# Another route to the low weights, and the rounded FFN activations on ScalarE outside the main heads

## The chip, the cores and the metric

One core of one Trainium2 chip. The metric is device microseconds of one execution, the median of three runs. The engines are TensorE (PE in the profile, its weight loads PEld), VectorE (DVE), ScalarE (ACT), GpSimd (POOL) and SyncE, whose queue (SPq) issues nearly all transfers. Each engine takes its instructions in the order in which they were laid down when the kernel was built.

## The reference

Forgetting attention, then a feed-forward net (FFN) over all tokens:

```python
scores = scale * np.matmul(q, k.transpose(0, 1, 3, 2))      # 8 batches x 8 heads, S=576, D=64
cum = np.cumsum(np.log(np.clip(f, 0.0001, 1.0)), axis=-1)
scores = scores + cum[:, :, :, None] - cum[:, :, None, :]    # causal
attn = softmax(scores);  x = attn @ v                        # tokens 4608 x 512
h = x @ w_in;  g = np.maximum(0.01 * h, h)                   # w_in 512 x 2048
out = g @ w_out                                              # w_out 2048 x 512
```

w_in and w_out are float64.

## The kernel before

The large products run as fp32r matmuls on pairs of a rounded high part and a low part: h is the sum of xh·win_h, xh·win_l and xl·win_h; o, the output, that of gh·wout_h, gh·wout_l and gl·wout_h, where gh is g rounded to fp32r and gl = g − gh.

**The weights** come in 16 pieces of 128 x 1024 (even numbers w_in, odd ones w_out), each as pairs of int32 words of the float64: `hi` (sign, exponent, 20 mantissa bits) and `lo` (32 more). `fetch_weight` issues the two transfers of a piece (L163) into one of two `wraw` buffers; `load_weight` makes the high weights (win_h, wout_h) and the low ones (win_l, wout_l) with two ScalarE and five VectorE instructions (L177 to L191). A `wraw` buffer is free for piece n+2 when the last of them has run; `wt`, a single buffer, is free for piece n+1 when its last reader has.

**The first 145 us** (the loop over `steps`) run an early attention over the first 256 tokens of three batches: in each of 12 steps two heads' scores (`sce`, whose max and exponentials `ze` go over DVE L301 and ACT L305), the division by their sums (L313), transposes (`tre`, copied out by ACT L325 as `pte`), attention times values (`ave`), and its split into `xh` (ACT L338) and `xl` (DVE L339). One weight piece is converted in each of the first eight steps, two in each of the last four. After each step `fill` puts in FFN work from the generator `ffn` (`FQ` sets how much: none in the first four steps); `warm` matmuls on zeros stand in the first six steps.

**From about 145 to 1095 us** the main heads run (`heads[0]` is True), with FFN work between them; there gl is made by GpSimd. **After 1095 us** only FFN is left. `ffn` makes, for each of 18 groups of 256 tokens and 8 pieces of w_in: `h` (24 matmuls), `g` by ScalarE (L629), `gh` by VectorE (L632), `gl` (L634: by VectorE where heads[0] is False), and then the 12 `o` matmuls of the piece before it (`second`).

A scheduler in the framework lays down the order on each engine when the kernel is built, from dependencies and its own estimate of durations; so a change of one instruction's engine or length can move others.

Of the kernel before, what the change touches and what calls it, by code (L numbers as in the profile page):

```python
# [8 lines left out]
F32 = mybir.dt.float32  # L9
F32R = mybir.dt.float32r  # L10
I32 = mybir.dt.int32
U32 = mybir.dt.uint32
AF = mybir.ActivationFunctionType
ALU = mybir.AluOpType
# [24 lines left out]
def forgetting_attention_ffn(ctx, tc, qT, kT, v4, vr, f, w_in, w_out, out):  # L39
# [6 lines left out]
    nc = tc.nc  # L46
# [60 lines left out]
    def matmul(*args, **kw):  # L107
        work[0] += 1
        nc.tensor.matmul(*args, **kw)  # L109
# [50 lines left out]
    def fetch_weight(n):  # L160
        raw = raws[n] = one.tile([P, 2, 4 * P, 2], I32, tag=RAWS[n % 2], name=f"wraw_{n}")
        for k, src in enumerate(wpieces[n][0]):
            nc.sync.dma_start(raw[:, k].rearrange("p w two -> p (w two)"), src)  # L163

    def load_weight(n):


        loaded.append(n)
        _, wh, wl = wpieces[n]
        wh, wl = (w.rearrange("p c f -> p (c f)") for w in (wh, wl))  # L170
        if n not in raws:
            fetch_weight(n)
        raw = raws[n].rearrange("p m w two -> p (m w) two")
        lo, hi = raw[:, :, 0], raw[:, :, 1]
        t = one.tile([P, 8 * P], I32, tag="vs", name=f"wt_{n}")
        tf = t.bitcast(F32)
        first = nc.scalar.activation(tf, hi.bitcast(F32), AF.Prelu, scale=REBIAS, alpha=SIGN)  # L177
        if n == 0:
            tc.keep_in_program_order(first)
        first = nc.vector.tensor_scalar(t, t, 3, None, op0=ALU.logical_shift_left)  # L180
        if n == 0:
            tc.keep_in_program_order(first)
        nc.scalar.copy(wh, tf)
        nc.vector.tensor_scalar(hi, t, -0x800000, None, op0=ALU.bitwise_and)
        rest = lo.bitcast(F32)
        nc.vector.scalar_tensor_tensor(
            rest, lo.bitcast(U32), 2.0**-52, hi.bitcast(F32), op0=ALU.mult, op1=ALU.mult
        )
        hi = hi.bitcast(F32)
        nc.vector.tensor_tensor(hi, tf, wh.bitcast(F32), op=ALU.subtract)  # L190
        nc.vector.tensor_tensor(wl, hi, rest, op=ALU.add)  # L191

    def weights(n):
        while len(loaded) < min(n, len(wpieces)):
            load_weight(len(loaded))
# [383 lines left out]
    def fetch_group(n):  # L579
        if n not in groups and n not in staged and (n + 1) * T <= ready[0]:  # L580
            xs = staged[n] = one.tile([P, NCC, T], F32R, tag="b4", name=f"xs_{n}", bufs=B4)
            since[n] = work[0]
            nc.sync.dma_start(xs.bitcast(F32), xd[:, n * T:(n + 1) * T].rearrange("(c p) t -> p c t", p=P))
# [8 lines left out]
    def ffn():  # L592
        pending = None
        half = NFC // 2
        order = [(0, 0, HP), (1, 0, HP), (0, HP, half), (1, HP, half)]
        order += [(n, 0, half) for n in range(2, NG)]
        for at, (n, p0, p1) in enumerate(order):
            while (n + 1) * T > ready[0]:
                yield False
            if n not in groups:  # L600
                if n not in staged:
                    fetch_group(n)
                near[0] = True
                while n not in groups:
                    yield False
            acc = [None, None]
            for p in range(p0, p1):
                while len(loaded) < 2 * (p + 1):
                    yield False
                near[0] = p == p1 - 1  # L610
                xh, xl = groups[n]
                terms = [
                    (x, c, w, xx) for c in range(NCC)
                    for x, (w, xx) in enumerate(((win_h[p], xh), (win_l[p], xh), (win_h[p], xl)))
                ]
                if n >= 2:
                    terms.sort(key=lambda y: y[0])
                ph = psum.tile([P, 2, T], F32, tag="h", name=f"h_{n}_{p}")
                for e in range(2):
                    fs = slice(e * P, (e + 1) * P)  # L620
                    for y, (x, c, w, xx) in enumerate(terms):
                        matmul(
                            ph[:, e, :], w[:, c, fs], xx[:, c, :],
                            start=y == 0, stop=y == len(terms) - 1,
                        )
                    if e == 0:
                        yield True
                g = one.tile([P, 2, T], F32, tag="b2", name=f"g_{n}_{p}", bufs=B2)
                nc.scalar.activation(g, ph, AF.Prelu, alpha=0.01)  # L629
                gh = one.tile([P, 2, T], F32R, tag="b2", name=f"gh_{n}_{p}", bufs=B2)  # L630
                gl = one.tile([P, 2, T], F32R, tag="b2", name=f"gl_{n}_{p}", bufs=B2)
                nc.vector.tensor_copy(gh, g)  # L632
                eng = nc.gpsimd if heads[0] else nc.vector
                eng.tensor_tensor(gl, g, gh.bitcast(F32), op=ALU.subtract)  # L634
                yield True
                if pending is not None:
                    yield from second(*pending)
                if p0 < p and at + 1 < len(order):
                    fetch_group(order[at + 1][0])
                pending = (n, p, p0, p1, gh, gl, acc)  # L640
        yield from second(*pending)

    def second(n, p, p0, p1, gh, gl, acc):
        for k in range(T // P):
            if p == p0:
                acc[k] = psum.tile([P, DM], F32, tag=f"o{k}", name=f"o_{n}_{k}_{p}", bufs=1)
            ts = slice(k * P, (k + 1) * P)
            for e in range(2):
                fc_ = 2 * p + e
                for x, (gg, w) in enumerate(((gh, wout_h[p]), (gh, wout_l[p]), (gl, wout_h[p]))):  # L650
                    matmul(
                        acc[k], gg[:, e, ts], w[:, e, :],
                        start=(fc_ == 2 * p0 and x == 0), stop=(fc_ == 2 * p1 - 1 and x == 2),
                    )
            if p == p1 - 1 < NFC // 2 - 1:
                tag, m = PARTS[2 * n + k]
                o = parts[n, k] = one.tile([P, DM], F32, tag=tag, name=f"part_{n}_{k}", bufs=m)
                nc.scalar.copy(o, acc[k])
            elif p == p1 - 1:
                if (n, k) in parts:  # L660
                    o = parts[n, k]
                    nc.vector.tensor_tensor(o, acc[k], o, op=ALU.add)
                else:
                    o = one.tile([P, DM], F32, tag="ost", name=f"ost_{n}_{k}", bufs=2)
                    nc.scalar.copy(o, acc[k])
                for x, row, m in segments(n * T // P + k):
                    nc.sync.dma_start(out[row:row + m, :], o[x:x + m])
            yield True

    parts = {}  # L670
    quanta = ffn()
    heads = [False]
    ready, used, credit = [0], [0], [0.0]
# [127 lines left out]
```

## Time and profile before

| | us |
|---|---|
| median of 3 runs (lowest, highest) | 1209.06 (1208.9, 1209.14) |
| the profiled execution: time, span in the profile | 1208.6, 1206.8 |
| busy in the span: PE, DVE, ACT, POOL | 1192.4, 625.9, 636.0, 461.0 |
| busy from 0 to 165 us: PE, DVE, ACT | 159.2, 126.8, 114.1 |

The profiled execution has 1.8 us outside the span, and the median of the runs is 0.46 us above it. Matmuls are pipelined and their ends are modelled, so a PE that is "busy" may still be held back. A group's idle time is the engine's idle time just before it.

### The profile page before, as it was taken

To read this page: it belongs to the slowest core of one execution; us is meant where nothing else is said; L and a number is where in the kernel's file an instruction comes from. 1 tells how busy PE (TensorE), PEld (TensorE's weight loads), DVE (VectorE), ACT (ScalarE), POOL (GpSimd) and SP (SyncE) were. 2 spreads that over 40 slices of the span, in tenths; PEclk is the share of its full clock that TensorE was granted. 3 is DMA by queue.
4 is the path that set the end of the run, shared out by engine and by line. 5 is a ranking of instruction groups with operands and counts; after the bars stand their busy time and mean duration, and the time that the engine had idled before them with its cause. 6 is when DMAs were issued, how large, how long until landed. Compare 5 with 4: busy or idle time off the path is not lost.

```text
span 1206.8 us, 22499 instructions
## 1 busy us (share of the span) xinstructions
PE 1192.4 (99%) x7812; PEld 1068.2 (89%) x7812; DVE 625.9 (52%) x1685; ACT 636.0 (53%) x1633; POOL 461.0 (38%) x473
## 2 busy tenths in 40 slices
PE   9999999999999999999999999999999999999998
PEld 6677888888899999999999999999999999998997
DVE  6988665565656555454445444444443434553221
ACT  5876665666755565555554545455444445552011
POOL 2000255555455445354435344444354543531000
PEclk9999999999999999999999999999999999999999
DMA  5555433334342333323332323232223222211000
GB/s 169 184 173 176 133 100 100 102 108 122 103 137 81 82 99 101 96 71 97 89 94 75 88 63 101 65 100 60 68 85 93 58 72 80 80 58 52 12 18 18
DMA packets 82129, 110.55 MB, mean 92 GB/s; under 512 B 20640, under 2 KB 51728, under 8 KB 82016
## 3 DMA queue, kind: packets, MB, share of 16 engines
q1 hardware_dynamic: 82016, 109.12, 31.0%
q8 instruction: 62, 1.02, 0.3%
q14 instruction: 51, 0.42, 0.1%
HBM read 65.32 MB, written 18.58 MB: 70 GB/s over the span
## 4 chain that ended last, share of the span: by engine, by line
PE 92%; DVE 2%; DMA 2%; ACT 2%; issue 1%; SPq 0%; POOL 0%; ACTq 0%; DVEq 0%; POOLq 0%
PE h L109 33%; PE o L109 32%; PE tr L113 8%; PE av L109 8%; PE sc L109 7%; PE sce L109 2%; DMA wraw<-in_w_in 2%; PE warm L109 2%; PE ave L109 1%; DVE fixed_z L412 0%; ACT wt L177 0%; PE tre L113 0%; ACT g L629 0%; DVE gh L632 0%; DVE pl L464 0%
## 5 line engine op out<-in xcount | busy, mean ns | idle before, releaser
L634 POOL TENSOR_TENSOR gl<-g,gh 128x512 fp32r<-128x512 f32 x113 | 148.7, 1316 | 275.6 <-DVE gh L632 270.7
L109 PE MATMUL o<-wout_h,gh 128*128 128x512 f32 x576 | 231.3, 402 | 0.0
L109 PE MATMUL o<-wout_h,gl 128*128 128x512 f32 x576 | 227.0, 395 | 0.6 <-DVE gl L634 0.6
L109 PE MATMUL o<-wout_l,gh 128*128 128x512 f32 x576 | 227.1, 394 | 0.0
L418 ACT ACTIVATE fixed_z<-fixed_z,max 128x192 f32<-128x192 f32 (+3 forms) x272 | 161.0, 592 | 100.3 <-DVE max L412 98.1
L109 PE MATMUL h<-xh,win_h 128*128 128x256 f32 x1152 | 206.5, 286 | 0.5 <-ACT xh L338 0.4
L462 ACT CAST ph<-tr 128x192 fp32r<-128x192 f32 (+3 forms) x360 | 126.9, 373 | 151.5 <-PE tr L113 99.5
L109 PE MATMUL h<-xh,win_l 128*128 128x256 f32 x1152 | 200.7, 283 | 0.0
L412 DVE CUSTOM_DVE_ANT_0 fixed_z<-sc,tri 128x192 f32<-128x192 f32 (+3 forms) x272 | 122.5, 452 | 150.6 <-PE sc L109 147.7
L629 ACT ACTIVATE g<-h 128x512 f32<-128x512 f32 x144 | 85.8, 596 | 214.6 <-PE h L109 202.9
L632 DVE CAST gh<-g 128x512 fp32r<-128x512 f32 x144 | 74.4, 517 | 209.8 <-ACT g L629 208.4
L464 DVE TENSOR_TENSOR pl<-tr,ph 128x384 fp32r<-128x384 f32 (+3 forms) x296 | 137.6, 467 | 82.2 <-ACT ph L462 81.1
L109 PEld LDWEIGHTS h<-xh,win_h 128*128 128x128 f32 x1152 | 170.9, 190 | 7.1 <-ACT xh L338 1.2
L109 PEld LDWEIGHTS h<-xh,win_l 128*128 128x128 f32 x1152 | 165.1, 191 | 0.8 <-DVE win_l L191 0.3
L109 PE MATMUL h<-xs,win_h 128*128 128x256 f32 x1024 | 164.4, 283 | 0.0
L113 PE MATMUL tr<-ident_r,fixed_z 128*128 128x128 f32 x888 | 145.2, 273 | 3.2 <-DVE ph L469 1.7
L109 PEld LDWEIGHTS h<-xs,win_h 128*128 128x128 f32 x1024 | 140.9, 191 | 0.0
L109 PEld LDWEIGHTS o<-wout_h,gl 128*128 128x128 f32 x576 | 108.2, 188 | 25.1 <-DVE gl L634 0.8
L113 PEld LDWEIGHTS tr<-ident_r,fixed_z 128*128 128x128 f32 x888 | 107.8, 140 | 24.6 <-ACT rb L541 5.2
L109 PEld LDWEIGHTS o<-wout_l,gh 128*128 128x128 f32 x576 | 108.7, 189 | 15.6 <-issue 0.2
L109 PEld LDWEIGHTS o<-wout_h,gh 128*128 128x128 f32 x576 | 108.9, 189 | 14.8
L109 PE MATMUL sc<-m,s 128*128 128x288 f32 (+1 forms) x336 | 120.6, 364 | 0.2
(111 smaller groups left out, 1684.4 us busy)
## 6 DMA issues: line engine op xcount, KB each, us to landing
raw<-in_kT SPq DMA_DIRECT2D x64, 144.0 KB
m<-m SPq DMA_DIRECT2D x64, 144.0 KB
wraw<-in_w_in SPq DMA_DIRECT2D x16, 512.0 KB
wraw<-in_w_out SPq DMA_DIRECT2D x16, 512.0 KB
fixed_vm<-in_v SPq DMA_DIRECT2D x64, 128.0 KB
xs<-xd SPq DMA_DIRECT2D x16, 512.0 KB
out<-ost SPq DMA_DIRECT2D x28, 256.0 KB
raw<-in_qT SPq DMA_DIRECT2D x40, 144.0 KB
```

Of the source, the lines that this page charges most:

```text
L109: nc.tensor.matmul(*args, **kw)
L113: nc.tensor.transpose(*args)
L412: nc.vector.tensor_tensor_reduce(out=z[:, a:b], in0=ps[:m, :b - a], in1=tri[:m, at:at + b - a], scale=-SCALE, scalar=3.0e38 if x == 0 else ...
L418: nc.scalar.activation(z, z, AF.Exp, bias=h["max"][:m, last:last + 1], scale=-1.0, accum_out=fixed["sum" + "ab"[s // 2 % 2]][:m, i, s % 2: ...
L462: nc.scalar.copy(strided(ph, run), source(ps, run))
L464: nc.vector.tensor_tensor(strided(pl, run), source(ps, run), strided(ph, run).bitcast(F32), op=ALU.subtract)
L629: nc.scalar.activation(g, ph, AF.Prelu, alpha=0.01)
L632: nc.vector.tensor_copy(gh, g)
L634: eng.tensor_tensor(gl, g, gh.bitcast(F32), op=ALU.subtract)
```

## The change

`load_weight` makes the low weights in another way. Before, the rest of rounding (tf − wh) and the scaled low word were computed apart and added. Now bit 2 is set in `t` (it stands for half of what `t` cuts off), the 9 lowest bits of `hi` and the 23 highest of `lo` are joined to one signed 32-bit integer, and this is multiplied by 2^-43 and the power of two of the weight. There are again five VectorE instructions, but of other kinds: before two of one input and three of two; now three of one input and two of two. The low weights no longer read the high ones.

`ffn` makes `gh` with ScalarE's copy where `heads[0]` is False (31 of 144 pieces: 12 ahead of the main heads, 19 behind them) and by VectorE otherwise.

```diff
-        first = nc.vector.tensor_scalar(t, t, 3, None, op0=ALU.logical_shift_left)
+        first = nc.vector.tensor_scalar(
+            t, t, 3, 4, op0=ALU.logical_shift_left, op1=ALU.bitwise_or
+        )
...
         nc.scalar.copy(wh, tf)
+        nc.vector.tensor_scalar(hi, hi, 23, None, op0=ALU.logical_shift_left)
+        nc.vector.scalar_tensor_tensor(
+            lo, lo, 9, hi, op0=ALU.logical_shift_right, op1=ALU.bitwise_or
+        )
         nc.vector.tensor_scalar(hi, t, -0x800000, None, op0=ALU.bitwise_and)
-        rest = lo.bitcast(F32)
         nc.vector.scalar_tensor_tensor(
-            rest, lo.bitcast(U32), 2.0**-52, hi.bitcast(F32), op0=ALU.mult, op1=ALU.mult
-        )
-        hi = hi.bitcast(F32)
-        nc.vector.tensor_tensor(hi, tf, wh.bitcast(F32), op=ALU.subtract)
-        nc.vector.tensor_tensor(wl, hi, rest, op=ALU.add)
+            wl, lo, 2.0**-43, hi.bitcast(F32), op0=ALU.mult, op1=ALU.mult
+        )
...
-                nc.vector.tensor_copy(gh, g)
+                (nc.vector.tensor_copy if heads[0] else nc.scalar.copy)(gh, g)
```

Lines behind L184 stand two further down in the new kernel (L185 is ScalarE's copy to the high weights; L186, L187, L190 and L191 are VectorE's new steps; L301 becomes L303, L629 L631, L634 L636, and the new L634 is gh). The order of the instructions moves on all engines up to the end of the early steps; from the first main head on it is the same on PE, DVE, ACT, POOL and SP, but for gh in the tail. Three places:

VectorE in the fourth early step (batch 0, head pair 3), before. Piece 2 is win_1; `xl_0_154<-ave_0_1` is the second quarter of xl of the first token group. Rows carry tile numbers.

```order
L186 SCALAR_TENSOR_TENSOR wraw_2_367<-wraw_2_367 128x1024
L301 ISA ze_1_0_0_504,maxe_1_0_496<-sce_1_0_0_498,tri_157 128x128
L301 ISA maxe_1_0_496 128x1
L190 TENSOR_TENSOR wraw_2_367<-wt_2_370,win_h_1_99 128x1024
L339 TENSOR_TENSOR xl_0_154<-ave_0_1_407,xh_0_153 128x256
L191 TENSOR_TENSOR win_l_1_107<-wraw_2_367 128x1024
L224 TENSOR_SCALAR fc_143<-fc_143 128x576
```

The same place now:

```order
L180 TENSOR_SCALAR wt_2_370<-wt_2_370 128x1024
L186 TENSOR_SCALAR wraw_2_367<-wraw_2_367 128x1024
L187 SCALAR_TENSOR_TENSOR wraw_2_367<-wraw_2_367 128x1024
L190 TENSOR_SCALAR wraw_2_367<-wt_2_370 128x1024
L191 SCALAR_TENSOR_TENSOR win_l_1_107<-wraw_2_367 128x1024
L226 TENSOR_SCALAR fc_143<-fc_143 128x576
L341 TENSOR_TENSOR xl_0_154<-ave_0_1_407,xh_0_153 128x256
```

All five steps of piece 2 now stand in a row, and xl is behind them, no longer between them.

ScalarE where the first FFN pieces come in (batch 1, head pairs 0 and 1), before:

```order
L629 ACTIVATE g_0_0_593<-h_0_0_568 128x512
L305 ACTIVATE ze_1_1_0_643,sume_1_1_636<-ze_1_1_0_643,maxe_1_1_635 128x128
L305 ACTIVATE ze_1_1_2_646,sume_1_1_636<-ze_1_1_2_646,maxe_1_1_635 128x128
L177 ACTIVATE wt_5_680<-wraw_5_677 128x1024
L183 CAST wout_h_2_116<-wt_5_680 128x1024
L629 ACTIVATE g_0_1_624<-h_0_1_599 128x512
L305 ACTIVATE ze_1_1_1_660,sume_1_1_636<-ze_1_1_1_660,maxe_1_1_635 128x256
L305 ACTIVATE ze_1_1_3_663,sume_1_1_636<-ze_1_1_3_663,maxe_1_1_635 128x256
L325 COPY pte_1_0_0_692<-tre_1_0_0_688 128x384
L325 COPY pte_1_0_1_698<-tre_1_0_1_694 128x384
```

The same place now:

```order
L631 ACTIVATE g_0_0_593<-h_0_0_568 128x512
L307 ACTIVATE ze_1_1_0_643,sume_1_1_636<-ze_1_1_0_643,maxe_1_1_635 128x128
L634 CAST gh_0_0_595<-g_0_0_593 128x512
L307 ACTIVATE ze_1_1_2_646,sume_1_1_636<-ze_1_1_2_646,maxe_1_1_635 128x128
L177 ACTIVATE wt_5_680<-wraw_5_677 128x1024
L327 COPY pte_1_0_0_692<-tre_1_0_0_688 128x384
L631 ACTIVATE g_0_1_624<-h_0_1_599 128x512
L307 ACTIVATE ze_1_1_1_660,sume_1_1_636<-ze_1_1_1_660,maxe_1_1_635 128x256
L307 ACTIVATE ze_1_1_3_663,sume_1_1_636<-ze_1_1_3_663,maxe_1_1_635 128x256
L185 CAST wout_h_2_116<-wt_5_680 128x1024
L327 COPY pte_1_0_1_698<-tre_1_0_1_694 128x384
L634 CAST gh_0_1_626<-g_0_1_624 128x512
```

gh is a new row, the first pte moves ahead of g, and the high weights' copy moves behind it, ahead of the second pte.

VectorE where pieces come two to a step (piece 10 is win_5; batch 2, head pair 1), before:

```order
L301 ISA ze_2_1_0_1129,maxe_2_1_1121<-sce_2_1_0_1123,tri_157 128x128
L301 ISA maxe_2_1_1121 128x1
L301 ISA ze_2_1_2_1132,maxe_2_1_1121<-sce_2_1_2_1124,tri_157 128x128
L301 ISA maxe_2_1_1121 128x1
L180 TENSOR_SCALAR wt_10_1156<-wt_10_1156 128x1024
L184 TENSOR_SCALAR wraw_10_1153<-wt_10_1156 128x1024
L634 TENSOR_TENSOR gl_1_0_1052<-g_1_0_1049,gh_1_0_1051 128x512
```

The same place now:

```order
L180 TENSOR_SCALAR wt_10_1156<-wt_10_1156 128x1024
L186 TENSOR_SCALAR wraw_10_1153<-wraw_10_1153 128x1024
L187 SCALAR_TENSOR_TENSOR wraw_10_1153<-wraw_10_1153 128x1024
L190 TENSOR_SCALAR wraw_10_1153<-wt_10_1156 128x1024
L303 ISA ze_2_1_0_1129,maxe_2_1_1121<-sce_2_1_0_1123,tri_157 128x128
L303 ISA maxe_2_1_1121 128x1
L303 ISA ze_2_1_2_1132,maxe_2_1_1121<-sce_2_1_2_1124,tri_157 128x128
L303 ISA maxe_2_1_1121 128x1
L191 SCALAR_TENSOR_TENSOR win_l_5_111<-wraw_10_1153 128x1024
L636 TENSOR_TENSOR gl_1_0_1052<-g_1_0_1049,gh_1_0_1051 128x512
```

Four of the five steps of piece 10 have moved ahead of the maxima of the step's scores; in SP's queue the transfers of piece 10 have moved from behind the loads of the first main head to right behind those of piece 9.

## The prediction, made before the changed kernel ran

> **What bounds the kernel now.** I read the page first, then busy times by stage, then PE's waits, and then the chain and the queues of the stages where PE waits. The page:
>
> ```profile
> span 1206.8 us, 22499 instructions
> ...
> PE 1192.4 (99%) x7812; PEld 1068.2 (89%) x7812; DVE 625.9 (52%) x1685; ACT 636.0 (53%) x1633; POOL 461.0 (38%) x473
> ```
>
> PE is busy in 99% of the span; 14.4 us are left in which it stands. The stages (start:end, length, then busy time and instructions of PE, PEld, DVE, ACT, POOL, then PE's granted clock, DMA share, GB/s):
>
> ```profile
> 0.00:165.00 165.00, 159.15 (x919) 124.21 (x920) 126.79 (x280) 114.06 (x272) 23.00 (x42) 0.99 0.50 163
> 165.00:1095.00 930.00, 925.09 (x6218) 846.54 (x6217) 473.52 (x1362) 507.09 (x1337) 433.24 (x430) 1.00 0.31 87
> 1095.00:1207.00 112.00, 108.20 (x681) 97.48 (x679) 25.59 (x43) 14.88 (x25) 4.80 (x2) 0.99 0.08 26
> 35.00:50.00 15.00, 13.38 (x65) 8.86 (x65) 13.42 (x32) 12.75 (x33) 0.00 (x0) 0.89 0.57 173
> 93.00:100.00 7.00, 6.35 (x36) 4.52 (x35) 4.32 (x12) 5.15 (x13) 0.00 (x0) 1.00 0.50 179
> 109.00:114.00 5.00, 4.25 (x27) 2.89 (x26) 3.36 (x8) 3.70 (x8) 0.00 (x0) 1.00 0.61 213
> 127.00:130.00 3.00, 2.31 (x15) 1.51 (x14) 2.93 (x8) 2.46 (x6) 0.88 (x4) 1.00 0.82 278
> ```
>
> Up to 165 us PE stands for 165 − 159.15 = 5.85 us; VectorE is busy 126.8 and ScalarE 114.1, so neither fills the stage, and what the change can move there is PE's waits. From 35 to 50 us PE stands for 15 − 13.38 = 1.62 us and has 0.89 of its clock, another 0.11 x 15 = 1.65. In the last three rows, 0.65, 0.75 and 0.69 are lost. In the other stages 4.9 and 3.8 us are lost; the order of no engine changes in the main heads, so I leave them as they are. PE's own waits (us in total, times, longest) name those who end them:
>
> ```profile
> PE ave L109 <- ACT pte L325: 0.9, 2, 0.6
> ...
> PE sce L109 <- DVE maxe L301: 0.8, 1, 0.8
> PE tre L113 <- DVE xl L339: 0.7, 2, 0.4
> PE o L109 <- DVE gl L634: 0.6, 1, 0.6
> ```
>
> All four are small steps of the early stage that stand in a queue behind conversions of weights.
>
> **The change, part by part.** First the sizes, from the groups of 0 to 165 us (count, then busy us and mean ns, then idle before) and two from all of ScalarE:
>
> ```profile
> L186 DVE SCALAR_TENSOR_TENSOR wraw<-wraw 128x1024 f32<-128x1024 uint32 x16 | 19.6, 1222 | 0.3
> ...
> L184 DVE TENSOR_SCALAR wraw<-wt 128x1024 int32<-128x1024 int32 x16 | 11.0, 688 | 0.3
> L180 DVE TENSOR_SCALAR wt<-wt 128x1024 int32<-128x1024 int32 x16 | 11.0, 688 | 3.3 <-ACT wt L177 3.3
> ...
> L190 DVE TENSOR_TENSOR wraw<-wt,wout_h 128x1024 f32<-128x1024 f32 x8 | 10.1, 1266 | 1.6 <-ACT wout_h L183 1.2
> ...
> L190 DVE TENSOR_TENSOR wraw<-wt,win_h 128x1024 f32<-128x1024 f32 x8 | 9.8, 1223 | 0.1
> ...
> L191 DVE TENSOR_TENSOR win_l<-wraw 128x1024 fp32r<-128x1024 f32 x8 | 9.7, 1216 | 0.0
> ...
> L183 ACT CAST win_h<-wt 128x1024 fp32r<-128x1024 f32 x8 | 8.4, 1047 | 1.9 <-DVE wt L180 1.8
> ...
> L632 DVE CAST gh<-g 128x512 fp32r<-128x512 f32 x14 | 6.8, 489 | 9.2 <-ACT g L629 8.8 <-ACT pte L325 0.2
> ```
>
> ```profile
> L374 ACT CAST m<-raw 64x576 fp32r<-64x576 f32 x64 | 43.0, 671 | 1.8 <-DMA raw<-in_kT 0.2
> ...
> L462 ACT CAST ph<-tr 128x512 fp32r<-128x512 f32 x64 | 37.4, 584 | 12.0 <-PE tr L113 11.0
> ```
>
> *VectorE, per piece.* Out go 688 + 688 + 1222 + 1245 (mean of 1266 and 1223) + 1216 = 5059 ns. In come L180 with a second operation in it, and the mask, both as before at 688; two of two inputs at 1222 (L187, L191); and the shift of `hi`, which reads every other word. No row reads one input with such a stride; the bounds are 688 (L184, which writes with that stride) and 1222. I take 688, since L184 is the nearer row: 4508 ns, 0.55 us less per piece, 8.8 us in 16. At 1222 the saving is 0.02 us per piece. [...]
>
> *gh.* 12 casts leave VectorE ahead of the heads, 12 x 0.49 = 5.9 us. On ScalarE one costs between 584 ns (512 columns out of PSUM, L462) and 671 (576 columns, L374); from 1047 at 1024 columns and 671 at 576, 0.84 ns a column gives 617 at 512, which I take: 12 x 0.62 = 7.4 us. So by 165 us VectorE goes from 126.8 to 112, ScalarE from 114 to 121.5. gl no longer waits across engines for VectorE's own cast but for ScalarE's; in the early stage its `o` stands a whole FFN piece behind `h`, and that piece's matmuls hide the 0.13 us.
>
> *The start, 33 to 48 us.* The chain of waits there, in order of time (start, us, what), then VectorE's queue and one row of PE (the `ave` of the fourth head pair; start, us, engine, line):
>
> ```profile
> 38.75 0.38 DVE fc L224
> ...
> 40.40 5.87 DMA wraw<-in_w_in
> ...
> 46.38 1.17 ACT wt L177
> ...
> 47.93 0.27 ACT xh L338
> ...
> 48.24 0.74 PE h L109 x4
> ```
>
> ```profile
> 33.83 1.25 DVE L186 SCALAR_TENSOR_TENSOR wraw<-wraw 128x1024 f32<-128x1024 uint32 x1
> ...
> 36.06 1.22 DVE L190 TENSOR_TENSOR wraw<-wt,win_h 128x1024 f32<-128x1024 f32 x1
> 37.20 0.42 DVE L339 TENSOR_TENSOR xl<-ave,xh 128x256 fp32r<-128x256 f32 x1
> ```
>
> ```profile
> 45.23 1.56 PE L109 MATMUL ave<-pte,ve 128*64 128x256 f32 x8
> ```
>
> xh of the fourth head pair is ready at 48.2, behind the conversion of piece 4 (L177), which waited for its transfer until 46.38. In the new order L177 of piece 4 stands behind this xh and two exponentials. The `ave` that it copies out is then the last before it: it ended at 45.23 + 1.56 = 46.8, and with 0.27 for xh, h could start 1.1 us sooner. Against this, `xl` (37.20) stands now behind all of piece 2, and no longer between its steps. Piece 2 begins now behind the last maximum of the pair, which VectorE had done at 33.83: five steps and `fc` take 4.51 + 0.38 = 4.9, so xl comes at 38.7, 1.5 us later. PE stands there longer, but two pieces' savings (1.1 us) come ahead of the next xl. In SP's queue the second transfer of piece 4 (40.40) has moved behind the last stores of the decay rows and a load of v, so L177 of piece 4 comes later; behind it wait the division of the next scores and the first g, not xh any more. I take −0.9. Ends: −3.3, if idle time and half clock both go (1.62 + 1.65), and +1.5, if xl's delay lasts.
>
> *50 to 62 us.* ScalarE's queue where gh comes in:
>
> ```profile
> 55.10 1.05 ACT L183 CAST wout_h<-wt 128x1024 fp32r<-128x1024 f32 x1 [0.88 <-DVE wt L180]
> 56.05 0.59 ACT L629 ACTIVATE g<-h 128x512 f32<-128x512 f32 x1
> ...
> 57.53 0.84 ACT L325 COPY pte<-tre 128x384 f32<-128x384 f32 x2
> ```
>
> ```profile
> 58.35 0.94 PE L109 MATMUL ave<-pte,ve 128*64 128x256 f32 x8
> ```
>
> The two `pte` (57.53, two copies) come one after the other and `ave` follows at 58.35 with no wait. Now the second `pte` has in front of it, besides what it had, one gh (0.62) and the copy of the high weights with its own wait (1.05 + 0.88) where it stood before g: at most 2.55 us later. Between the halves of `ave` the new PE order has seven `o` (7 x 0.233 = 1.6, by the 24 in 5.59 us of the tail's row below): 0.9 is left, which I take; ends 0 and +2.6. The wait is new: what stands behind the second `pte` are the other gh, the division of the next pair's scores, and xh.
>
> *75 to 145 us.* Three waits (0.65, 0.75, 0.69 in the stage rows): `o` for a gl that VectorE took up behind L180 and L184 of piece 10, scores for a maximum behind L180 and L184 of piece 12, `ave` for a `pte` behind L183 of piece 14. The pieces are converted sooner now, with 0.55 us less each, and gh is not in VectorE's way; but four steps of piece 10 and the first of piece 13 stand ahead of maxima that stood ahead of them. I take half, −1.0; ends −2.1 and +1.0.
>
> *The tail.* There gh adds to a chain that PE covers:
>
> ```profile
> 1197.71 0.60 ACT L629 ACTIVATE g<-h 128x512 f32<-128x512 f32 x1 [5.05 <-PE h L109]
> ```
>
> ```profile
> 1198.34 0.43 DVE L632 CAST gh<-g 128x512 fp32r<-128x512 f32 x1 [4.42 <-ACT g L629]
> 1198.87 0.69 DVE L634 TENSOR_TENSOR gl<-g,gh 128x512 fp32r<-128x512 f32 x1
> ```
>
> ```profile
> 1197.62 5.59 PE o L109 x24
> ```
>
> The last g ends at 1198.31; with 0.62 for gh and 0.69 for gl, gl is ready at 1199.7. PE has 12 `o` of the piece before until 1197.62 + 2.79 = 1200.4. Cost 0, as long as 0.7 us of cover last; every earlier piece has the next `h` besides.
>
> Sum: −0.9 + 0.9 − 1.0 = −1.0. The profiled execution, 1206.8 + 1.8 outside, becomes 1207.6; the median of the runs was 0.46 above it, so 1208.1.
>
> **Rivals.** (Under 0.2%, 2.4 us, a measurement of this kernel hardly tells a change from none.)
>
> *ScalarE becomes what PE waits for: slower.* It gets 7.4 us in the 95 us from 50 on, in a queue in which L177 stands waiting for transfers at any place the scheduler chose; each gh in front of a `pte`, `xh` or exponential that PE needs costs 0.62. It decides if about half of the 12 do and the other savings fail: 6 x 0.62 = 3.7, so 1212.8. For it speaks that before, too, `pte` and xh were the waits of PE; against it, that ScalarE was idle for 51 of 165 us.
>
> *The waits close: faster.* The idle time of 35 to 50 and the three later waits go, 1.62 + 2.06, and the second `pte` is hidden: 1209.1 − 3.7 = 1205.4. VectorE's 14.7 us less speak for it; against it, that each wait has an order behind it and not only a load.
>
> *The clock holds: faster.* From 35 to 50 it was 0.89. With the new order's −1.0 and no slow stretch, −2.65: 1206.4. [...]
>
> *The strided shift takes 1222: the change saves VectorE nothing.* Then the start gives −0.3, the later waits 0: 1209.1 + 0.6 = 1209.7.
>
> **How the numbers follow.** The forecast, 1208.1 (own range 1206.7 to 1210.5), 42%; the slow shift, 7%; both within 0.2%. Waits that close, 23%, and the held clock, 10%, are faster. ScalarE, 18%, is slower. So faster 0.33, same 0.49, slower 0.18. The ends of the terms give 1209.1 − 5.4 = 1203.7 and 1209.1 + 5.1 = 1214.2, which need all to fall one way; 8 times in 10 I expect 1204.4 to 1212.3.
>
> **What would show it.** Right: L186 and L190 near 690 ns, gh on ScalarE near 620; PE idle by 165 us near 5; h of the fourth quarter before 47.5; a wait of `ave` for `pte` near 59; the rows after the first main head as before, moved by one amount. Wrong: PE standing for ScalarE several times between 50 and 145, a second stretch of half clock, or new waits in the main heads.

## The result, and the profile after

The changed kernel takes 1215.39 us (median of 6 runs, 1213.86 to 1216.07) against 1209.10 (6 runs, 1208.13 to 1210.84): 1.0052 of the time before, 95% interval 1.0041 to 1.0063. It is 6.3 us slower, outside the range of the forecast. The profiled execution took 1216.07, with a span of 1214.3. Its page:

```profile
span 1214.3 us, 22482 instructions
...
PE 1199.4 (99%) x7812; PEld 1072.6 (88%) x7812; DVE 604.0 (50%) x1654; ACT 653.8 (54%) x1664; POOL 460.8 (38%) x473
```

PE executes the same 7812 instructions, and its busy time has grown from 1192.4 to 1199.4 us: nearly the whole loss is PE being longer at the same work, not PE waiting. A lower clock counts in this busy time too (an h matmul takes 0.42 us at 47.25 us, at half clock, and 0.28 at 52.29), so the two rows alone don't tell why. The stages (start:end, length, busy time and instructions of PE, PEld, DVE, ACT, POOL, PE's granted clock, DMA share, GB/s):

```profile
0.00:165.00 165.00, 158.59 (x868) 121.52 (x869) 111.73 (x258) 115.86 (x272) 18.51 (x36) 0.96 0.49 158
35.00:50.00 15.00, 12.77 (x53) 8.55 (x54) 12.16 (x28) 10.78 (x29) 0.00 (x0) 0.72 0.71 222
50.00:62.00 12.00, 12.00 (x68) 8.86 (x66) 8.02 (x19) 9.73 (x25) 0.00 (x0) 0.93 0.24 81
112.00:118.00 6.00, 5.07 (x38) 4.27 (x36) 2.25 (x3) 2.35 (x3) 0.00 (x0) 1.00 0.90 319
118.00:124.00 6.00, 5.37 (x23) 3.93 (x24) 5.83 (x15) 5.19 (x13) 0.00 (x0) 0.72 0.05 21
165.00:1095.00 930.00, 925.18 (x6218) 847.10 (x6218) 474.34 (x1367) 508.43 (x1341) 435.75 (x434) 1.00 0.31 88
```

Up to 165 us PE stands for 6.4 us (5.85 before), at a clock of 0.96 (0.99 before). The main heads are as before (925.18 beside 925.09). From 35 to 50 us PE now loses 15 − 12.77 = 2.2 us and has 0.72 of its clock; from 118 to 124 the clock is down a second time. Half clock (a granted clock of 0.50) lasts from 41.5 to 51.8 us, 10.24 us or three windows of 3.41, and from 120.1 to 123.5, one more; before there was one, of 3.41 us, near 38 us. Matched by the same matmul, this trace is 3.5 us later than that of before at about 52 us (the last h of FFN piece 1), 5.5 at 63, 7.4 where the main heads begin, and 7.5 at the end. PE's longer waits:

```profile
PE ave L109 <- ACT pte L327: 1.6, 1, 1.6
PE sce L109 <- DVE maxe L303: 1.6, 1, 1.6
...
PE h L109 <- ACT win_h L185: 0.9, 1, 0.9
```

The sizes of the parts (groups of 0 to 165 us: count, then busy us, mean ns):

```profile
L190 DVE TENSOR_SCALAR wraw<-wt 128x1024 int32<-128x1024 int32 x16 | 11.1, 692 | 0.2
L186 DVE TENSOR_SCALAR wraw<-wraw 128x1024 int32<-128x1024 int32 x16 | 11.0, 687 | 0.0
...
L634 ACT CAST gh<-g 128x512 fp32r<-128x512 f32 x12 | 7.4, 620 | 3.2 <-PE o L109 1.6 <-issue 1.5
```

The strided shift takes 687 ns and the mask 692; gh on ScalarE takes 620, where I had taken 688 and 617. The two long waits in their queues, first ScalarE's and PE's at 39 us (start, us, engine, line; in brackets the idle time before and who ended it):

```profile
39.13 1.14 ACT L177 ACTIVATE wt<-wraw 128x1024 f32<-128x1024 f32 x1
40.15 0.69 ACT L209 CAST fcq<-start 128x576 fp32r<-128x576 f32 x1
40.71 0.88 ACT L327 COPY pte<-tre 128x384 f32<-128x384 f32 x2
```

```profile
41.27 1.92 PE L109 MATMUL ave<-pte,ve 128*64 128x256 f32 x8 [1.57 <-ACT pte L327]
```

The copies of the transposes (pte, 40.71) stand behind the conversion of weight piece 3 (L177) and a row of the decay vectors (L209), and `ave` behind them. And at 117 us, ScalarE, VectorE, PE:

```profile
116.51 1.13 ACT L177 ACTIVATE wt<-wraw 128x1024 f32<-128x1024 f32 x1 [3.25 <-DMA wraw<-in_w_out]
```

```profile
117.67 0.69 DVE L180 TENSOR_SCALAR wt<-wt 128x1024 int32<-128x1024 int32 x1 [3.70 <-ACT wt L177]
118.28 0.28 DVE L303 CUSTOM_DVE_ANT_0 ze<-sce,tri 128x128 f32<-128x128 f32 x1
```

```profile
118.63 0.70 PE L109 MATMUL sce<-qk 64*128 64x256 f32 x3 [1.56 <-DVE maxe L303]
```

ScalarE stands 3.25 us for the transfer of piece 13, VectorE 3.70 for ScalarE, and the maxima (118.28) wait behind VectorE's L180, though their scores were there at about 116.7. PE waits 1.56 for them.

### The profile page after: what moved, and what is told of

It reads as the page before. It is cut to its first block, busy times and chain, and to the rows that moved or that the text cites. A ratio compares the mean times of both kernels' runs of the same rounds, so it can differ in the third digit from the quotient of the medians.

```text
span 1214.3 us, 22482 instructions
## 1 busy us (share of the span) xinstructions
PE 1199.4 (99%) x7812; PEld 1072.6 (88%) x7812; DVE 604.0 (50%) x1654; ACT 653.8 (54%) x1664; POOL 460.8 (38%) x473
## 4 chain that ended last, share of the span: by engine, by line
PE 95%; DVE 2%; ACT 2%; DMA 1%; issue 1%; POOL 0%; SPq 0%; ACTq 0%; DVEq 0%; POOLq 0%
PE h L109 33%; PE o L109 32%; PE tr L113 8%; PE av L109 8%; PE sc L109 7%; PE sce L109 2%; PE warm L109 2%; PE ave L109 1%; PE tre L113 1%; DMA wraw<-in_w_out 0%; DVE fixed_z L414 0%; ACT g L631 0%; ACT wt L177 0%; DVE pl L466 0%; DVE gh L634 0%
## 5 line engine op out<-in xcount | busy, mean ns | idle before, releaser
L636 POOL TENSOR_TENSOR gl<-g,gh 128x512 fp32r<-128x512 f32 x113 | 148.4, 1313 | 276.2 <-DVE gh L634 271.1
L631 ACT ACTIVATE g<-h 128x512 f32<-128x512 f32 x144 | 85.7, 595 | 204.0 <-PE h L109 196.8
L634 DVE CAST gh<-g 128x512 fp32r<-128x512 f32 x113 | 59.3, 525 | 130.4 <-ACT g L631 129.0
L150 POOL TENSOR_TENSOR fixed_m2a<-raw,m 64x576 fp32r<-64x576 f32 x32 | 46.6, 1457 | 201.9 <-ACT m L376 184.9
```

What stands on the lines that cost most here:

```text
L150: nc.gpsimd.tensor_tensor(out, a, b, op=ALU.subtract)
L634: (nc.vector.tensor_copy if heads[0] else nc.scalar.copy)(gh, g)
```

## The experiments

Kernels that were run together share the runs of the kernel before; I compare by the ratio to these. Where an order is held, edges that carry no wait fix the order in which an engine issues, so that the other parts of the kernel can be exchanged under it:

```python
ORDERS = {"PE": ((69, 20), ...), "DVE": ..., "Activation": ..., "SP": ...}   # the first 145 us
traced = {i.name: i for i in nc.cur_bb.bb.instructions}
...
for engine, runs in ORDERS.items():
    names = [f"I-{s + x}" for s, n in runs for x in range(n)]
    for x, y in zip(names, names[1:]):
        ...
        tc.add_manual_dep(traced[y], x, info, reason="order")   # issue order only
```

**Which part, and is it the clock?** My first theory (A) was that PE has little work near 38 us and pays for it in half clock. The first two runs take the parts alone.

```diff
 # e1: the changed kernel, but
-(nc.vector.tensor_copy if heads[0] else nc.scalar.copy)(gh, g)
+nc.vector.tensor_copy(gh, g)
 # e2: the kernel before, but
-nc.vector.tensor_copy(gh, g)
+(nc.vector.tensor_copy if heads[0] else nc.scalar.copy)(gh, g)
```

> The new low weights alone; gh stays on VectorE everywhere. The order of every engine is that of the changed kernel up to about 52 us. Theory A (the new order of the weights' steps makes PE thin near 38 us, and half clock costs the time): PE waits again about 1.6 us near 40 us for pte, three windows of 3.41 us at half clock follow, and the time is 1212.5 to 1215.5. Theory B (the added gh fill ScalarE's queue and cause the loss): no second slow stretch, 1207.5 to 1209.5.

> gh by ScalarE ahead of and behind the main heads alone; the old low weights. The order of every engine is that of the kernel before up to about 62 us. Theory A: the one window of half clock near 38 us as before, 1208 to 1210.5. Theory B: new waits of PE for pte, xh or the exponentials behind gh, 1212 to 1216.

The weights alone: 1213.61 us, 1.0042 [1.0027, 1.0057]. gh alone: 1208.65, 1.0000 [0.9990, 1.0009]. The loss comes in with the weights; ScalarE's added casts cost nothing by themselves. The next two put filler matmuls into this place, in the changed kernel and in the one before.

```diff
 # early_values, head pair 2 (counted from 0), ahead of its ave
+pad = ...   # the bank of PSUM that is free until the first o
+for _ in range(10):
+    matmul(pad[:, :T], still[:, :P], xh[:, 1, :], start=True, stop=True)
```

> The changed kernel with ten matmuls of 256 columns whose result nobody reads, between the transposes of the third head pair, where PE has 1.6 us without work; the order of VectorE, ScalarE and the queues is unchanged, and PE's differs only there. Theory A: the three windows of half clock from 41.5 us go, 5.1 us, and at most 0.6 comes back where the ten (1.2 us) don't fit into the wait: 1209.8 to 1211.5; the later window near 120 us stays. Theory that the waits themselves cost the time and the clock is incidental: 1215 to 1217.

> The kernel before with the same ten matmuls at the same place. Theory A: its one window of half clock near 38 us goes, -1.7 us, against up to 1.2 us for the ten where they stand ahead of work: 1207.4 to 1208.9, with a granted clock of 1.00 from 30 to 60 us. If the clock doesn't matter: 1209 to 1210.4.

Changed kernel: 1213.85, 1.0043 [1.0028, 1.0058]. Kernel before: 1208.72, 0.9996 [0.9986, 1.0005]. In the kernel before the window of half clock went (a granted clock of 1.00 up to 165 us, 0.99 without the fillers), and the time stayed: PE stood 2.3 us for pte, 0.9 before. In the changed one a window of the three went and two stayed (0.97 up to 165 us, 0.96 without the fillers), so the test was weak. e8 repeats it with orders held, twelve fillers right in the wait and six in the next one.

```diff
 # PE's order
+pad x12
 ave (head pair 2)
 ...
+pad x6
 ave (head pair 3)
```

> The changed kernel, all orders held as they are, with twelve matmuls of 256 columns that nobody reads straight ahead of the third head pair's ave, in the wait of 1.6 us, and six ahead of the fourth's. Theory A (half clock costs the time from 41 to 52 us): at full clock PE would stand some 0.7 us for pte in place of 5.1 us lost; 1210.5 to 1212.5, granted clock 1.00 from 40 to 52 us. Rival (ScalarE's and VectorE's chain sets the time there and the clock only fills PE's waits): 1214.5 to 1216.5.

1214.09, 1.0042 [1.0027, 1.0056]. The stretches from 38 to 52 us, of this run and, behind it, of the changed kernel:

```profile
38.10:41.50 3.40, 3.24 (x27) 2.76 (x26) 3.31 (x10) 3.40 (x6) 0.00 (x0) 1.00 0.87 261
41.60:51.70 10.10, 9.38 (x64) 7.24 (x62) 7.72 (x21) 8.03 (x23) 0.00 (x0) 1.00 0.66 211
```

```profile
38.10:41.50 3.40, 1.73 (x10) 1.30 (x11) 3.31 (x12) 3.36 (x8) 0.00 (x0) 1.00 0.85 265
41.60:51.70 10.10, 10.07 (x35) 6.52 (x33) 6.08 (x16) 5.16 (x15) 0.00 (x0) 0.50 0.68 211
```

The clock held, and x64 instructions (six of them fillers) ran where x35 had run; the last h of FFN piece 2 stands 3.9 us sooner (0.5 of it from the start). But of this only 1.4 is left at the end of the span, and the median moved by about 1.2. It was given back at the wait for maxe (2.3 us for 1.6) and in two places of the main heads, near 160 and 257 us. So half clock was real, and taking its three windows away brought little of the loss back. The test is not clean: the eighteen fillers are work as well, and the waits moved. Theory A falls as the one cause; what half clock costs in this order is left open.

**The order, not the steps.** e5 gives the new weights the order of before, e6 the old weights the new order; no instruction differs from e1 and from the kernel before.

```diff
 # e5: the new low weights, gh by VectorE;  e6: the kernel before
+ORDERS = ...   # e5: the order of the kernel before;  e6: the order of e1
```

> The new low weights alone, with the order of every engine held to that of the kernel before, row for row (the five VectorE steps of a piece stand where the five old ones stood). Theory O (the order that the scheduler chose for the new steps costs the time, not the steps): 1206.5 to 1209.5, at most one window of half clock near 38 us. Rival (the new steps themselves disturb the other engines): 1212 to 1215, as with the new weights in their own order.

> The old low weights (all of the kernel before), with the order of the engines held to the one that the new weights alone gave. Theory O: 1213 to 1216, with two or three windows of half clock after 38 us; more than the new weights in the same order, if anything, as each piece takes 0.55 us longer on VectorE. Rival: 1207.5 to 1210.

e5: 1207.60, 0.9983 [0.9973, 0.9994]. e6: 1215.86, 1.0058 [1.0043, 1.0073]. This settles the first question: the new steps save 1.6 to 2 us, and the order that came with them costs 7 or more. e9 takes up the second wait, the one for maxe.

```diff
 # VectorE's order                      # ScalarE's likewise: L177 and L185 of piece 13
-L180 of piece 13                       # behind the exponentials and pte
 maxima of 128 columns, twice
-L186, L187 of piece 13
 gl; maxima of 256 columns, twice
+L180, L186, L187 of piece 13
 L190, L191 of piece 13
```

> The changed kernel, all orders held, but for the conversion of weight piece 13, whose transfer comes late: on VectorE its five steps stand behind the four maxima and the gl that they stood ahead of or between, on ScalarE its two behind the exponentials and pte copies. If VectorE's standing for this transfer costs the second loss near 118 us: the wait of 1.6 us for maxe and the window of half clock near 120 us go, 1.6 + 1.7, and up to 1 comes back: 1212.0 to 1213.5. If another wait takes its place: 1214.5 to 1216.

1214.59, 1.0046 [1.0031, 1.0061]: 0.7 under the changed kernel, which the intervals don't tell from nothing, and not 2 to 3.4. VectorE's wait went, and PE stood for gl (1.2) and for maxe (0.7) in its place.

**Where in the order.** The whole change with all orders held (e7), and three that change from one order to the other on the way.

```diff
+ORDERS = ...   # e7: the order of gh alone (e2), throughout
+               # e10: that up to head pair 3's ave, then the changed one;  e11: the reverse
+               # e12: that up to head pair 0's ave, then the changed one
```

> The whole change (new low weights, gh by ScalarE outside the main heads), all orders held to those that the scheduler chose for the gh part alone, which are those of the kernel before up to 62 us. Theory O (only the order costs): 1206.5 to 1209. If the two parts together disturb each other in any order: 1212 to 1216.

> The whole change; the rows up to the fourth head pair's ave (154 of PE, 69 of VectorE, 59 of ScalarE, 37 of SP; to about 46 us) in the order of the run above, the rest in the changed order. If both places of loss count by themselves, the late one alone is left, 2 to 3 us: 1210 to 1211.5. If the early loss is taken up later anyway (the transfers of weights set the pace): 1213 to 1215. If the early order is all that costs: 1207 to 1209.

> The mirror of the run above: the changed order up to the fourth head pair's ave, the order of the run with all held for the rest. Both places count: the early loss alone, 3.5 to 5 us over that run, 1211 to 1213.5. Taken up later: 1207.5 to 1209.5. The early order is all: 1213.5 to 1216.

> The whole change; only the rows up to the first head pair's ave and what stands beside it (94 of PE, 37 of VectorE, 32 of ScalarE, to about 29 us) in the held order, where the changed one has the next scores and six fillers ahead of that ave's second half and ScalarE's conversion of piece 2 comes 1.5 us later; the rest in the changed order. If this first difference is the root of the early loss: near the run with rows to 46 us, 1210 to 1212. If the later rows are: 1214.5 to 1216.

e7: 1208.00, 0.9992 [0.9982, 1.0001]. e10: 1211.87, 1.0020 [1.0006, 1.0034]. e11: 1209.11, 1.0006 [0.9996, 1.0016]. e12: 1214.01, 1.0049 [1.0031, 1.0066]. The early order with its waits and half clock costs 1.7 us over e7, the rows behind 46 us 3.4, both together 7.3; with these intervals the 2 us beyond the sum may be chance. The first 30 us are not the root. The surprise is e10, whose page stands below that of e7:

```profile
span 1204.2 us, 22484 instructions
...
PE 1189.4 (99%) x7812; PEld 1066.7 (89%) x7812; DVE 605.0 (50%) x1654; ACT 654.6 (54%) x1664; POOL 461.2 (38%) x473
```

```profile
span 1208.2 us, 22486 instructions
...
PE 1193.4 (99%) x7812; PEld 1068.2 (88%) x7812; DVE 605.5 (50%) x1654; ACT 654.4 (54%) x1664; POOL 461.1 (38%) x473
```

Neither has a stretch of half clock up to 165 us (a granted clock of 1.00 in both), and both stand some 6 us up to 165 us; all of the 4.0 us is PE's busy time, for the same 7812 instructions. So PE's instructions cost different amounts in different neighbourhoods.

**Pairs.** A step of the early attention does two heads. Their scores read 64 rows of the array each (`64*128` in PE's rows), and the two halves of `ave` write 64 columns each (`128*64`). In the order of before most pairs stand side by side; the changed order puts other rows between. e14 does this to e7 at five places with nothing else moved, e13 undoes it in the changed kernel at six; ave of head pair 4 (head pairs are counted from 0 here and in what was expected of the last six runs; the first, e8's, e10's and the mirror's expectations count from 1):

```diff
 # e14, PE's order                       # e13 does the reverse
 ave<-pte_1_0_0  x2
-ave<-pte_1_0_1  x2
 o<-wout_h,gl; o<-wout_h,gh; o<-wout_l,gh; o<-wout_h,gl
+ave<-pte_1_0_1  x2
 h ...
```

> The changed kernel, all orders held, but PE's: four ave (of head pairs 4, 5, 7 and 8) and two pairs of scores (of head pair 5), whose two halves stand apart with FFN rows or fillers between, are put together, at the place of the later half. Theory J (a pair that stands apart takes PE about 0.6 us longer an ave and 0.5 longer a pair of scores): 4 x 0.6 + 2 x 0.5 = 3.4 less, 1211.5 to 1213. If the rows between hide it, or only waits count: 1214.5 to 1216.5.

> The whole change in the held order, with three ave (head pairs 4, 5, 7) and the two pairs of scores of head pair 5 parted by four to six rows of PE's own next work, as the changed order parts them; nothing else moves and no row is new. Theory J: 3 x 0.6 + 2 x 0.5 = 2.8 more than the 1208.0 of the held order: 1210 to 1211.5. If only waits count: 1207 to 1209.

PE's rows there in e7, and below in e14 (in the `ave` rows each product counts as two instructions):

```profile
56.87 0.40 PE L183 MATMUL o<-wout_l,gh 128*128 128x512 f32 x1
57.25 1.24 PE L183 MATMUL ave<-pte,ve 128*64 128x256 f32 x8
58.42 0.50 PE L183 MATMUL o<-wout_h,gl 128*128 128x512 f32 x1
58.76 0.39 PE L183 MATMUL o<-wout_h,gh 128*128 128x512 f32 x1
58.99 0.39 PE L183 MATMUL o<-wout_l,gh 128*128 128x512 f32 x1
...
59.46 0.28 PE L183 MATMUL h<-xh,win_h 128*128 128x256 f32 x1
59.58 0.28 PE L183 MATMUL h<-xh,win_l 128*128 128x256 f32 x1
```

```profile
59.48 0.40 PE L203 MATMUL o<-wout_l,gh 128*128 128x512 f32 x1
59.86 0.86 PE L203 MATMUL ave<-pte,ve 128*64 128x256 f32 x4
60.65 0.51 PE L203 MATMUL o<-wout_h,gl 128*128 128x512 f32 x1
61.00 0.39 PE L203 MATMUL o<-wout_h,gh 128*128 128x512 f32 x1
...
61.46 0.40 PE L203 MATMUL o<-wout_h,gl 128*128 128x512 f32 x1
61.78 0.86 PE L203 MATMUL ave<-pte,ve 128*64 128x256 f32 x4
62.58 0.39 PE L203 MATMUL h<-xh,win_h 128*128 128x256 f32 x1
62.80 0.28 PE L203 MATMUL h<-xh,win_l 128*128 128x256 f32 x1
```

From the o ahead of it to the second h behind it, the same rows take 59.58 − 56.87 = 2.71 us in e7 and 62.80 − 59.48 = 3.32 in e14: 0.61 more, with no wait. Joined, both halves of ave take 58.42 − 57.25 = 1.17; apart, 0.79 and 0.80, so side by side they overlap for a good part. Besides, an o starts 0.34 to 0.35 behind the start of the o that follows ave, where it takes 0.23 otherwise, and ave starts 0.32 or 0.38 behind an o's start; from these starts I estimate about 0.1 for each change between the two forms.

e14: 1210.92, 1.0012 [1.0002, 1.0023], 2.4 us over e7, for 2.8 expected. e13: 1210.17, 1.0003 [0.9989, 1.0018], 5.9 us under the changed kernel, for 3.4 expected. Not all of the 5.9 is the joining. In the profiled runs the last h of FFN piece 1, which stands ahead of the first joined row, starts at 56.24 us in the changed kernel and at 54.18 in e13, where one window of half clock fewer came (0.76 of the clock from 38 to 52 us, for 0.63): 2.1 of the 4.8 us between the two spans (1214.3 and 1209.5) were there already, and 2.7 come behind. e14 against e7, read in the same way, gives 53.34 − 51.55 = 1.8 ahead of the first parted row, again with one window of half clock (0.99 of the clock up to 165 us, for 1.00), and 3.2 behind it. Runs of one mean clock say about the same: at 0.996, three runs of e13 have 1211.1 and two of the changed kernel 1214.0; at 0.994, one has 1213.3 and four have 1215.7.

So the parted pairs cost some 3 us of the 7.3, by both runs and near the 2.8 and 3.4 that were expected (of the six in e13, ave of head pair 8 is parted in e7 too, so e14's five are those that count here). This is the largest cause that the runs show apart, and it is about what e10 lost behind 46 us (3.4), where all of them stand. The early place costs 1.7 by e11. What is left, some 2 us, lies within the intervals or goes with half clock and the waits of the early order; the runs don't divide these. In e13 the three runs with a mean clock of 0.999 have a median of 1207.0, the seven with 0.994 to 0.997 have 1211.1; what else differs between these executions is not known.

**What is to be had.** e15 joins five pairs that e7's own order parts; e16 adds e9's edit to e13.

```diff
 # e15, PE's order (head pair 3; also ave of 0 and 8, scores of 3 and 4 at two more places)
-sce_0_3_0<-qk; sce_0_3_0<-both
 tre ...
+sce_0_3_0<-qk
 sce_0_3_2<-qk
+sce_0_3_0<-both
 sce_0_3_2<-both
```

> The whole change in the held order, with the pairs that it parts itself put together: two ave (head pairs 0 and 8) and the scores of head pairs 3 and 4 at three places. Theory J where PE is what the rest waits for: up to 2 x 0.6 + 3 x 0.5 = 2.7 less, but four of the five stand ahead of 46 us, where PE waits for ScalarE and VectorE anyway: 1206 to 1207.5. If a joined pair makes its first half late for VectorE and ScalarE: 1208 to 1209.5.

> The changed kernel with both: the six pairs joined and weight piece 13 converted behind the maxima and exponentials, where it doesn't hold them up. If the two late causes are separate, what is left over the held order is the start, about 1.7: 1209.5 to 1211.5. If one is the other's consequence: 1211.5 to 1213.

e15: 1205.57, 0.9967 [0.9953, 0.9982]. e16: 1211.58, 1.0014 [1.0002, 1.0027], no better than e13: once the pairs stand together, nothing is gained that can be seen by moving piece 13 out of the way. The last two have one joined order on every engine, with the new and with the old weights.

```diff
 # e18: e5, e19: the kernel before; in both
+ORDERS = ...   # the order of before; ave of 0 and 5, scores of 3 and 4 at three places joined
```

> The new low weights alone (gh by VectorE), in the order of the kernel before with five of its parted pairs joined (ave of head pairs 0 and 5, scores of head pairs 3 and 4 at three places). If the gain of the held and joined whole change is arithmetic plus pairs: 1204.5 to 1206.5. If gh by ScalarE has a part in it: 1206.5 to 1208.

> The kernel before with the same five pairs joined and nothing else: old low weights, gh by VectorE, all other rows where they were. If the pairs alone bring the gain: 1205 to 1206.5, as the run beside it. If the shorter VectorE steps bring what they brought without joining (1.5 us): 1206.5 to 1208. If the pairs ahead of 46 us are hidden by waits with the old steps: 1208 to 1209.5.

e18: 1205.84, 0.9970 [0.9960, 0.9981]. e19: 1206.68, 0.9986 [0.9977, 0.9995]. The new arithmetic is worth 1.9 us in the joined order (0.0016), as 2.0 without (0.9983 against 1); joining is worth about 1.6; gh by ScalarE nothing that shows (0.9967 with it, 0.9970 without). e15 and e18 beat both kernels of this case. e15's page:

```profile
span 1202.1 us, 22483 instructions
...
PE 1187.3 (99%) x7812; PEld 1066.2 (89%) x7812; DVE 605.4 (50%) x1654; ACT 653.9 (54%) x1664; POOL 460.8 (38%) x473
```

PE's busy time is 5.1 us less than before, in the same instructions; each of the two profiled runs has one window of half clock near 40 us (0.99 of the clock up to 165 us).

## Why the prediction was wrong

*Sizes of the instructions.* Right: 687 and 692 ns against 688, 620 against 617. One sum slipped: the three later waits add up to 2.09 us, not 2.06, which leaves 1205.4 as it is.

*The step that failed.* I let a moved PE row cost the same wherever it stands. In the term from 50 to 62 us I had the evidence in hand: "Between the halves of `ave` the new PE order has seven `o`", and I counted these seven as cover for a late pte. The wait that they were to cover did not come (PE stands for nothing from 50 to 62 us), and the parting itself cost (0.61 us a pair in e14's rows); by the same matmuls the stretch from 52 to 63 us lost 1.9 us, for the 0.9 forecast, by another cause. That the sign was right here is luck. In all, rows parted in this way cost some 3 us that no term of the sum had; the start, below, is the other part of the miss.

*The start, −0.9 forecast, +3.5 measured at 52 us.* I looked for xl to be late, and hoped for h sooner. pte was late instead, behind L177 of piece 3, which I had left out, and so was win_h (0.9 us). Then three windows of half clock came where one had been, and h of the fourth quarter began at 52.07, not before 47.5. e11 shows that this place costs about 1.7 us at the end, less than at 52 us.

*75 to 145 us, −1.0 forecast, +1.9 measured.* The old waits of 0.65 and 0.69 went, as I thought. I had seen "the first of piece 13" move ahead of the maxima and gave it no price, though behind it stood ScalarE's wait for a transfer: 1.56 and one more window of half clock. By e9 and e16 the wait itself is not what the time is lost to, since another takes its place. Two `ave` (head pairs 7 and 8) that stood joined in the kernel before are parted in this stretch; at e14's 0.6 each, an estimate, they are 1.2 us.

*The tail, 0.* Right: the difference is 7.4 us at the first main head and 7.5 at the end.

*The rivals.* "ScalarE becomes what PE waits for" came nearest in time (1212.8) and was wrong as a mechanism: the gh casts cost nothing (e2), and where PE did wait for ScalarE (pte 1.6, win_h 0.9), no gh stood in front. "The clock holds" was wrong in sign; of the signs that I had listed against myself, a second stretch of half clock came. "The waits close" needed VectorE's savings without a new order: e5 gives 1.6 us of its 3.7. None of the cases held that the order could make PE's own work longer, so none reached 1215.

## What to carry to other kernels

When a shorter step lets a scheduler lay down all engines anew, price the new order as well as the step: first compare the busy time of the engine that sets the time, at the same number of instructions and the same granted clock. Look at where products that use half of the array stand: here rows of other work between the halves of one `ave` cost 0.6 us (e14). A new step is tried fairly only under a held order; here that turned the new weights' loss of 5 us into a gain of 2, and joining pairs made it 3.6.

## What was not expected of the hardware

In these traces two halves of the array worked side by side when their rows were neighbours in PE's order, and not when four other rows stood between: 1.17 us (e7) against 0.79 + 0.80 = 1.59 (e14) for one `ave`.

In the traces of before and of the changed kernel half clock came, up to 165 us, in stretches of 3.41 us or a multiple of it (3.41 near 38 us before; 10.24 and 3.41 in the changed kernel), behind stretches in which PE waited no longer than 1.6 us at a time; in e8 its longest wait was 2.3 (for maxe), with a granted clock of 0.79 from 112 to 118 us. Ahead of the three windows PE was busy for 1.73 of 3.40 us (the row 38.10:41.50 above), and ahead of the one of before for more:

```profile
34.50:37.80 3.30, 2.90 (x16) 1.78 (x16) 2.53 (x6) 2.86 (x12) 0.00 (x0) 1.00 0.43 119
```

These runs don't show what brings half clock on.

Less clock did not go with as much more time. Over 103 runs of the kernel before, those with a mean clock of 0.999 or more have a median of 1208.46 (61 runs), those with 0.996 or less 1209.63 (22), and the 20 between them 1209.68: 1.2 us for at least 0.003 x 1207 = 3.6 us of lost clock. e4 shows one way in which this can be: with the clock held, PE waited 1.4 us longer for ScalarE in the same place. In e13 about as much lost clock went with 4.1 us. These are comparisons between executions; only e4 and e8 held the clock by an edit, and that gained nothing in e4 and 1.2 us in e8.
